# Four of six query groups in packed float32, values of two units and packed scores grouped, sink probabilities placed by VectorE, masks alone on GpSimd

## The chip, the cores and the metric

The kernel runs on one core of a Trainium2 chip. The metric is the device time of one execution in microseconds; three runs of the kernel before took 628.79 to 629.53 us, with a median of 629.14 us. Five engines share the work: TensorE (PE in the profile; PEld is its loading of weights), VectorE (DVE), ScalarE (ACT), GpSimd (POOL) and SyncE (SP, which here issues the DMAs).

## The reference

Attention with a sliding window of 128 keys and 4 sink keys, for 2 batches of 8 heads, 768 positions and a head dimension of 64, all in float32. Its output, 1536 rows of 512, goes through two feed-forward layers (512 to 2048 and back): the first with a leaky ReLU, the second with SiLU.

```python
keep = is_sink | ((rel >= 0) & (rel < window))
scores = np.where(keep, q @ k.T / sqrt(D), -1e9)
a = np.exp(scores - scores.max(-1)); a = a / (a.sum(-1) + 1e-9)
x = heads_beside_each_other(a @ v)                  # 1536 x 512
h = x @ w_in;  x = np.maximum(0.01 * h, h) @ w_out  # layer 1
h = x @ w_in2; y = (h / (1 + np.exp(-h))) @ w_out2  # layer 2
```

## The kernel before, in words

**Attention.** The 768 positions of a batch are cut into three query groups of 256, so there are six groups; `turns` puts the two first groups of the batches (g = 0, no keys before them) ahead of the other four. A unit is one pair of heads in one group: 4 units per group, 24 in all. A unit has two slots of 128 queries. `scores` (line 648) multiplies queries with at most 260 keys into the PSUM tiles `sc`; VectorE adds the mask, takes the row's extreme and writes `P`; ScalarE takes the exponential and the row's sum. `normalise` (683) divides by the sum: for g > 0 `P` itself is scaled, for g = 0 a scaled identity `by` is made, with which the transposing matmul multiplies. `transposes` (708) turns `P` around on TensorE (`tr`, for some slots the tile `h`) and ScalarE copies the result to `pT`. `values` (741) multiplies with v into the tile `at`, and ScalarE and VectorE split the result into a rounded part `xh` and its rest `xl`.

**Two forms of scores.** The first `WHOLE` = 3 groups in turn are "whole": q and k stay float32, and two heads, each 64 rows deep, are multiplied beside each other in the two halves of the array (profile form 64\*128). In the other groups q and k are split into a rounded part and a rest: ScalarE writes `qkh` (line 621), GpSimd `ql` (622), VectorE half of `qkh` (624), and the products run over 128 rows as float32r (form 128\*128). Value matmuls use half of the array's columns (128\*64). All the rest runs as 128\*128.

**Sinks.** For g > 0 the probabilities of the 4 sink keys go to `psink` as a rounded part, a rest, and the rounded part again: ScalarE, VectorE, ScalarE (703 to 705). They are transposed into `at`, and ScalarE copies two stripes of 32 rows to `sink_t` (739).

**Feed-forward.** Weights arrive as raw halves `wr` of 512 columns; ScalarE, VectorE (four operations), ScalarE and VectorE turn one into a rounded part and a rest, `w` or `we` (line 506 to 514). While attention runs, TensorE also works on 30 "items" (chunks of layer 1 for 256 positions): 12 matmuls to `h`, ScalarE and VectorE make `ga`, 12 matmuls to `ya`. After attention come 81 fused items of 512 positions: 12 matmuls to `h`, then `gb`, then 12 matmuls to four banks `y`, with `y` of an item two items behind its `h`. When a run of items over one block of positions ends, VectorE adds the four banks to `yp`.

**The order.** `Recorder` writes down every operation and then sets each engine's order by itself: it gives each operation a cost (`cost`, line 151) and a due time counted back from TensorE's order, and issues what can start first, ties by due time. Some operations may go to one of several engines (`scaled`, 235). All instructions are issued at line 441, so the profile shows that line everywhere and the names of tiles tell the operations apart.

Of the kernel before, what the change touches and what calls it, by code (L numbers as in the profile page):

```python
# [8 lines left out]
F32 = mybir.dt.float32  # L9
# [7 lines left out]
P = 128  # L17
# [4 lines left out]
WHOLE = 3  # L22
# [14 lines left out]
W_FIRST, W_EVERY = 1, 1.3  # L37

# [12 lines left out]
class View:  # L51
# [28 lines left out]

    def size(self):
        n = 1
        for a, b in self.box[1:]:
            n *= b - a
        return n
# [28 lines left out]
class Op:  # L114
    def __init__(self, eng, rank):
        self.eng, self.rank = eng, rank
        self.calls, self.cost, self.deps, self.opens, self.users = [], 0, {}, [], []
        self.bytes, self.port, self.mode = 0, False, None

        self.alts = {}  # L120


class Recorder:
# [7 lines left out]
    def __init__(self, tc):  # L131
# [3 lines left out]
        self.after = None  # L135
        for e in self.ENGINES:
            setattr(self, e, _Engine(self, e))
# [13 lines left out]
    def cost(self, eng, name, out, ins, kw):  # L151
        n = out.size() if isinstance(out, View) else 0
        psum = any(isinstance(a, View) and a.tile.pool.psum for a in [out, *ins])
        if eng == "tensor":
            passes = 4 if ins[0].dtype == F32 else 1

            half = name == "matmul" and min(out.box[0][1] - out.box[0][0], ins[0].box[0][1] - ins[0].box[0][0]) <= 64
            if name == "transpose":
                return max(109, n / 2.4)
            return n * passes / 2.4 * (0.5 if half else 1) + (20 if half else 13.3)  # L160
        if name == "dma_start":
            return 0
        if eng == "scalar":
            by = any(isinstance(kw.get(k), View) for k in ("scale", "bias"))
            sparse = isinstance(ins[0], View) and ins[0].tile.tag == "wr"
            return (182 if by else 51 if psum else 93) + n / 1.2 + (95 if "accum_out" in kw else 55 if sparse else 0)
        if eng == "vector":
# [3 lines left out]
            if name == "reciprocal":  # L171
                return 70 + n * 6
            return 68 + n / (0.96 if two or psum else 1.92)
# [15 lines left out]
    def add(self, eng, name, args, kw):  # L189
# [7 lines left out]
        else:  # L197
            op = Op(eng, self.rank - self.bias)
            op.i = len(self.ops)
            if self.after is not None:  # L200

                op.deps[self.after] = 0
            self.rank += 1
# [97 lines left out]
    def order(self):  # L301

        for op in self.ops:
            op.need, op.est = len(op.deps), 0.0
# [47 lines left out]
        while len(done) < len(self.ops):  # L352
# [33 lines left out]
            else:  # L386
                end = free[op.eng] = start + op.cost
                if op.eng == "tensor":

                    end = free[op.eng] = end + (95 if mode is not None and mode != op.mode else 0)  # L390
# [65 lines left out]
def attention_moe(ctx, tc, cfg, ins, out):  # L456
# [35 lines left out]
    def load_half(after=None):  # L492
# [5 lines left out]
        R.after = after  # L498
# [16 lines left out]
        R.after = None  # L515
# [32 lines left out]
    def emit_y(yps, gt, t, layer, c, first, last):  # L548
        cs = slice(c * P, (c + 1) * P)
        with R.group():  # L550
            for j, (a, b) in enumerate(((0, 0), (1, 0), (0, 1))):
                l, r = (wo(t, a)[:, cs], gt[:, b, :]) if layer == 0 else (gt[:, b, cs], wo(t, a))
# [4 lines left out]
    if near:  # L557
        mask = [attn.tile([P, 260], BF16, f"mask{i}") for i in range(4)]
        psink = [attn.tile([P, P], F32, f"psink{i}") for i in range(2)]
        sink_t = [attn.tile([P, GT], F32R, f"sink_t{i}") for i in range(2)]  # L560

# [40 lines left out]
    def load_qk(n):  # L602
# [19 lines left out]
        R.gpsimd.tensor_tensor(ql, raw[:, :, :GT], f32(hi[:, :, :GT]), op=ALU.subtract)  # L622
# [4 lines left out]
    def load_v(n):  # L627
# [7 lines left out]
        if d["g"] > 0 and key not in sinks:  # L635
            sr = attn.tile([P, P + 1], F32, "sr", 2)
            R.sync.dma_start(out=sr, in_=ins["vs"][key])

            sh = attn.tile([P, P], F32R, "sh", 1)
            R.vector.tensor_copy(sh, sr[:, :P])  # L640
            sinks[key] = attn.tile([P, P], F32R, "sk", NP + 1)
            R.vector.scalar_tensor_tensor(sinks[key], in0=f32(sh), scalar=sr[:, P:P + 1], in1=sr[:, :P],
# [5 lines left out]
    def scores(s):  # L648
# [10 lines left out]
        scs = {}  # L659
        if u["whole"]:  # L660

            scs = {j: ps_a.tile([P, 260], F32, "sc", 2) for j in range(2)}
            with R.group():
                for j, sc in scs.items():
# [3 lines left out]
        for j in range(2):  # L668
            if j in scs:
                sc = scs[j]  # L670
            else:
                sc = ps_a.tile([P, 260], F32, "sc", 2)
# [10 lines left out]
    def normalise(s):  # L683
# [5 lines left out]
        if d["u"]["whole"] and d["g"] == 0:  # L689

            d["by"] = attn.tile([P, 2, P], F32, "by", 3)
# [6 lines left out]
        if d["g"] > 0:  # L698
            s0 = 2 * P if i == 0 else P
            src = pt[:, :, s0:s0 + NS]  # L700
            hi, lo, hi2 = (psink[s // 2 % 2][:, o:o + 2 * NS].rearrange("p (j s) -> p j s", j=2)
                           for o in range(32 * i, 32 * i + 6 * NS, 2 * NS))
            R.scalar.activation(hi.bitcast(F32R), src, AF.Copy)
            R.vector.tensor_tensor(lo.bitcast(F32R), src, hi, op=ALU.subtract)
            R.scalar.activation(hi2, hi, AF.Copy)
        R.bias = 0

    def transposes(s):
# [16 lines left out]
        if i == 0:  # L725
            u["pT"] = attn.tile([P, 2, 512], F32, "pT", 2)
# [5 lines left out]
        u["at"] = ps.tile([P, 512], F32, "ya0", 1) if early and s // 2 % 2 else ps_a.tile([P, 512], F32, "at", 1)  # L732
        if g > 0:

            R.tensor.transpose(u["at"][:, 256:384], psink[s // 2 % 2], ident)
            st = u["st"] = sink_t[s // 2 % 2]
            for k in range(2):
                r = slice(32 * k, 32 * k + 32)
                R.scalar.activation(st[r, k * QB:(k + 1) * QB], u["at"][r, 256:384], AF.Copy)

    def values(n):

        u = state.pop(n)
        g, av, v, pT = u["g"], u["at"], u["v"], u["pT"]
        mm = [(1, 128, 384, 0), (0, 0, 128, 0), (2, 384, 512, 128)] if g > 0 else [(0, 128, 384, 0), (1, 384, 512, 128)]
        with R.group():
            if g > 0:
                R.tensor.matmul(av[:, 0:GT], sinks[u["G"] // NG, u["p"]], u["st"], start=True, stop=False)
            for k, (blk, a, e, o) in enumerate(mm):
                for j in range(2):  # L750
                    r = slice(D * j, D * j + D)
                    R.tensor.matmul(av[r, o:o + e - a], v[:, blk, r], pT[:, j, a:e],
                                    start=g == 0 and k == 0, stop=k == len(mm) - 1)
        T, t0 = divmod(u["G"] * GT, 512)
        x = [t[T][:, u["p"], t0:t0 + GT] for t in (xh, xl)]
        R.scalar.activation(x[0], av[:, 0:GT], AF.Copy)
# [294 lines left out]
```

## Time and profile before

| what | value |
|---|---|
| median of three runs | 629.14 us |
| profiled execution, its own time | 629.62 us |
| its span in the trace | 627.8 us |
| TensorE busy | 616.7 us, 98% of the span |
| VectorE, ScalarE, GpSimd busy | 400.7, 320.7, 29.4 us |
| granted TensorE clock | 1.0 (full speed) in every stretch shown |

The span begins at the first instruction and ends at the last one's end; the 1.8 us between it and the execution's own time lie outside. A busy TensorE in this profile is not TensorE at its peak: the end of a matmul is modelled, and a matmul that waits for room in the pipeline counts as busy. So for the stretch with attention one looks at the chain that ended last, and at what its pieces would take without waits.

### The profile page before, as it was taken

Reading aid. Unit: us, or ns where it says so; the run is one execution under the profiler, and the core shown is the slowest. Engines: PE = TensorE matmul, PEld = TensorE weight load, DVE = VectorE, ACT = ScalarE, POOL = GpSimd, SP = SyncE. Lnnn points to the kernel's source line nnn. Section 1 sums busy time; section 2 is a strip of 40 time slices with the busy share of each in tenths; the row PEclk is TensorE's granted clock in tenths of the full one; section 3 lists DMA queues with packets and bytes.
Section 4 is the critical chain, followed back from the end, with each engine's and each line's share of the span. In section 5 each row is a group of like instructions: output and inputs, shape, how many; then the busy total and the mean of one; then the engine's idle time right before and its main releaser. Section 6 shows DMA issues by size and latency. Waiting matters only on the chain.

```text
span 627.8 us, 9200 instructions
## 1 busy us (share of the span) xinstructions
PE 616.7 (98%) x3368; PEld 518.8 (83%) x3368; DVE 400.7 (64%) x984; ACT 320.7 (51%) x789; POOL 29.4 (5%) x44
## 2 busy tenths in 40 slices
PE   7899999999999999999999999999999999999997
PEld 5688888989998888888888888888888888888886
DVE  4998978788696666443646498874554644455254
ACT  5989999999764333332434256454323323332221
POOL 2002013320000000000000000000000000000000
PEclk9999999999999999999999999999999999999999
DMA  8544654331253212020010113220101010000013
GB/s 297 155 167 160 207 173 140 124 102 47 83 190 130 75 62 102 33 68 33 34 66 34 38 66 135 101 101 33 65 4 68 34 34 33 1 0 1 2 67 134
DMA packets 19341, 53.34 MB, mean 85 GB/s; under 512 B 2144, under 2 KB 6752, under 8 KB 19296
## 3 DMA queue, kind: packets, MB, share of 16 engines
q1 hardware_dynamic: 19296, 52.76, 24.6%
q8 instruction: 26, 0.43, 0.3%
q14 instruction: 19, 0.16, 0.1%
HBM read 49.61 MB, written 3.15 MB: 84 GB/s over the span
## 4 chain that ended last, share of the span: by engine, by line
PE 87%; ACT 10%; DVE 2%; issue 1%; DMA 0%; DVEq 0%; ACTq 0%
PE h L441 40%; PE y L441 35%; PE ya L441 5%; ACT P L441 4%; PE sc L441 3%; PE tr L441 2%; PE at L441 2%; ACT pT L441 2%; ACT qkh L441 1%; DVE P L441 1%; ACT psink L441 1%; ACT sink_t L441 1%; ACT ga L441 0%; ACT xh L441 0%; DMA qk<-in_qkd 0%
## 5 line engine op out<-in xcount | busy, mean ns | idle before, releaser
L441 PE MATMUL h<-xh,w 128*128 128x512 f32 (+1 forms) x600 | 157.2, 350 | 0.0
L441 ACT ACTIVATE g<-h 128x512 f32<-128x512 f32 (+1 forms) x111 | 59.6, 537 | 138.5 <-PE h L441 138.5
L441 PEld LDWEIGHTS h<-xh,w 128*128 128x128 f32 x600 | 104.7, 189 | 14.7 <-issue 0.8
L441 DVE TENSOR_TENSOR gb<-g,gb 128x512 fp32r<-128x512 f32 x81 | 55.9, 690 | 77.0 <-ACT g L441 61.2
L441 PE MATMUL h<-xl,w 128*128 128x512 f32 (+1 forms) x300 | 104.0, 347 | 0.0
L441 DVE TENSOR_TENSOR g<-g,h 128x512 f32<-128x512 f32 x48 | 33.0, 687 | 91.6 <-ACT g L441 91.6
L441 DVE SCALAR_TENSOR_TENSOR wb<-wr,wb 128x512 uint32<-128x512 uint32 x128 | 87.7, 689 | 2.8
L441 PE MATMUL h<-xh,we 128*128 128x512 f32 x288 | 88.7, 389 | 0.0
L441 ACT ACTIVATE gb<-h 128x512 fp32r<-128x512 f32 x33 | 19.7, 597 | 100.9 <-PE h L441 100.9
L441 PE MATMUL y<-we,gb 128*128 128x512 f32 x288 | 69.2, 389 | 0.0
L441 PE MATMUL y<-w,gb 128*128 128x512 f32 x288 | 68.9, 389 | 0.0
L441 PEld LDWEIGHTS y<-w,gb 128*128 128x128 f32 x288 | 54.1, 188 | 11.2
L441 PEld LDWEIGHTS y<-we,gb 128*128 128x128 f32 x288 | 54.1, 188 | 11.2
L441 PEld LDWEIGHTS h<-xh,we 128*128 128x128 f32 x288 | 54.1, 188 | 11.1
L441 PEld LDWEIGHTS h<-xl,w 128*128 128x128 f32 x300 | 56.7, 189 | 7.1
L441 ACT ACTIVATE P<-P,sm 128x260 f32<-128x260 f32 (+2 forms) x118 | 56.8, 492 | 7.5 <-DVE sm L441 7.3
L441 PE MATMUL y<-gb,w 128*128 128x512 f32 x252 | 60.5, 389 | 0.0
L441 PE MATMUL h<-xl,we 128*128 128x512 f32 x144 | 56.1, 390 | 0.0
L441 DVE TENSOR_SCALAR wb<-wb 128x512 f32<-128x512 f32 (+1 forms) x128 | 53.6, 424 | 3.6 <-ACT wb L441 2.2
L441 PEld LDWEIGHTS y<-gb,w 128*128 128x128 f32 x252 | 47.3, 188 | 9.8
L441 PE MATMUL ya<-ga,w 128*128 128x256 f32 x360 | 49.6, 286 | 0.0
L441 DVE TENSOR_TENSOR yp<-yp,y 128x512 f32<-128x512 f32 (+1 forms) x61 | 38.0, 673 | 14.7 <-PE y L441 14.7
(72 smaller groups left out, 767.4 us busy)
## 6 DMA issues: line engine op xcount, KB each, us to landing
wr<-in_w SPq DMA_DIRECT2D x64, 512.0 KB, 3.6
qk<-in_qkd SPq DMA_DIRECT2D x12, 644.0 KB, 3.9
v<-in_vd SPq DMA_DIRECT2D x16, 192.0 KB, 2.5
out_y<-yp SPq DMA_DIRECT2D x11, 256.0 KB, 2.1
qk<-in_qkd SPq DMA_DIRECT2D x4, 322.0 KB, 5.7
v<-in_vd SPq DMA_DIRECT2D x8, 128.0 KB, 3.5
qkh<-in_qkd SPq DMA_DIRECT2D x4, 256.0 KB, 6.7
qk<-in_qkd SPq DMA_DIRECT2D x3, 256.0 KB, 3.8
```

The source lines that it names most:

```text
L441: getattr(eng, name)(*[_real(x) for x in a], **{k: _real(x) for k, x in kw.items()})
```

## The change

- `WHOLE` goes from 3 to 4: a fourth group has packed float32 scores and no `qkh` or `ql`.
- For g = 0 both slots' scores of a unit go into one pair of PSUM banks, in one group of matmuls; units 1, 3 and 5 take the bank `ya1` for one of the pair.
- `values` handles two units at once, in one bank `at`, with one copy each to `xh` and `xl`.
- VectorE makes `sink_t` from the transposed sinks and a 0/1 mask `own`; ScalarE writes both rounded parts of `psink` in one operation.
- `ql` moves from GpSimd to VectorE, and `scaled` no longer offers GpSimd.
- The ordering gets new costs, and weight splits may not be planned more than 16 us (`HOLD`) before they are due.
- The last bank of the output is made in two halves in two banks, and the last half's store is issued by ScalarE.

```diff
-WHOLE = 3
+WHOLE = 4
+COLD = 11000
+HOLD = 16000.0
 ...
     def scaled(self, out, src, by, *more):
         self.either(("scalar", "activation", (out, src, AF.Copy), dict(scale=by)),
-                    ("vector", "tensor_scalar", (out, src, by, None), dict(op0=ALU.mult)),
-                    ("gpsimd", "tensor_scalar", (out, src, by, 1.0), dict(op0=ALU.mult, op1=ALU.mult)))
+                    ("vector", "tensor_scalar", (out, src, by, None), dict(op0=ALU.mult)))
 ...
+        for op in self.ops:
+            op.est = max(0.0, op.due - HOLD) if op.split else 0.0
 ...
-        R.gpsimd.tensor_tensor(ql, raw[:, :, :GT], f32(hi[:, :, :GT]), op=ALU.subtract)
+        R.vector.tensor_tensor(ql, raw[:, :, :GT], f32(hi[:, :, :GT]), op=ALU.subtract)
 ...
-        if u["whole"]:
-            scs = {j: ps_a.tile([P, 260], F32, "sc", 2) for j in range(2)}
+        if u["whole"] and g == 0:
+            if i == 0:
+                spare = {1: ["ya1", "sc"], 3: ["ya1", "sc"], 5: ["ya1", "sc"]}.get(s // 2, ["sc", "sc"])
+                u["sc"] = [ps_a.tile([P, 512], F32, t, 2) if t == "sc" else ps.tile([P, 512], F32, t, 1) for t in spare]
+            for blocks in ((i,),) if s < 2 else ((0, 1),) if i == 0 else ():
+                with R.group():
+                    for k in blocks:
+                        for j, sc in enumerate(u["sc"]):
 ...
-            R.scalar.activation(hi.bitcast(F32R), src, AF.Copy)
+            R.scalar.activation(twice.bitcast(F32R), src.repeat(1, [P, 2, 2, NS]), AF.Copy)
             R.vector.tensor_tensor(lo.bitcast(F32R), src, hi, op=ALU.subtract)
-            R.scalar.activation(hi2, hi, AF.Copy)
 ...
-            for k in range(2):
-                r = slice(32 * k, 32 * k + 32)
-                R.scalar.activation(st[r, k * QB:(k + 1) * QB], u["at"][r, 256:384], AF.Copy)
+            R.vector.tensor_tensor(st.rearrange("p (k n) -> p k n", k=2), u["at"][:, o:o + P].repeat(1, [P, 2, QB]),
+                                   own.rearrange("p (k n) -> p k n", k=2), op=ALU.mult)
 ...
     def values(n):
-        u = state.pop(n)
+        us = [state.pop(n + k) for k in range(2)]
 ...
+        x = [t[T][:, p:p + 2, t0:t0 + GT] for t in (xh, xl)]
+        both = av.rearrange("p (k n) -> p k n", k=2)
+        R.scalar.activation(x[0], both, AF.Copy)
+        R.vector.tensor_tensor(x[1], both, f32(x[0]), op=ALU.subtract)
 ...
+        ends = layer == 1 and final and T == NT - 1
+        parts = [(c, 0, 512) for c in range(KC - ends)] + ends * [(KC - 1, 0, 256), (KC - 1, 256, 512)]
 ...
+                R.vector.tensor_tensor(part, part, yp_k, op=ALU.add)
+                (R.scalar if o else R.sync).dma_start(out=out[r0:r0 + P, cols], in_=part)
```

On TensorE, the values of a late unit before (`at_2098` is the unit's bank; `sc` over `qkh` and `ql` are the float32r scores of the next unit):

```order
L441 MATMUL tr_2111<-ident_88,P_2008 128x128 x4
L441 MATMUL ya_5_1864<-ga_2006,w_696 128x256 x3
L441 MATMUL at_2098<-sink_t_0_138,sk_1623 128x256
L441 MATMUL at_2098<-pT_2043,v_1807 64x256 x2
L441 MATMUL at_2098<-pT_2043,v_1807 64x128 x4
L441 MATMUL sc_2145<-qkh_1957 128x260
```

On TensorE, the values of two late units in the changed kernel (`at_2054` holds both, `pT_2029` and `pT_2134` are the two units' probabilities):

```order
L463 MATMUL sc_2211<-qkh_2038 128x260
L463 MATMUL sc_2211<-qkh_2038,ql_2075 128x260
L463 MATMUL at_2054<-sink_t_0_811,sk_1015 128x256
L463 MATMUL at_2054<-sink_t_0_917,sk_1374 128x256
L463 MATMUL at_2054<-pT_2029,v_1808 64x256 x2
L463 MATMUL at_2054<-pT_2029,v_1808 64x128 x4
L463 MATMUL at_2054<-pT_2134,v_2010 64x256 x2
L463 MATMUL at_2054<-pT_2134,v_2010 64x128 x4
L463 MATMUL tr_2243<-ident_88,P_2088 128x128 x4
```

One run of half-column matmuls stands now where there were two, a unit later for the first of the pair. Over the whole program TensorE leaves the 128\*128 form 32 times instead of 38.

On ScalarE, a stretch of a late unit before (`psink` and `sink_t` are the sinks, `qkh` the split of a unit to come, `ga` and `g` belong to an item):

```order
L441 ACTIVATE psink_0_108<-P_2008 128x8
L441 ACTIVATE wb_2100<-wr_1068 128x512
L441 ACTIVATE sink_t_0_138<-at_2098 32x128 x2
L441 ACTIVATE psink_0_108<-psink_0_108 128x8
L441 ACTIVATE ga_2123<-h_2079 128x256
L441 ACTIVATE pT_2127<-tr_2111 128x2x256
L441 ACTIVATE g_2138<-h_2079 128x256
L441 ACTIVATE P_2053<-P_2053,sm_2054 128x260
L441 ACTIVATE P_2108,sm_2109<-P_2108,sm_2109 128x260
L441 ACTIVATE xh_0_1823<-at_2098 128x256
L441 ACTIVATE psink_0_108<-P_2053 128x8
```

On ScalarE, a like stretch of the changed kernel:

```order
L463 ACTIVATE pT_1911<-tr_1930 128x2x256
L463 ACTIVATE qkh_1955<-qk_69 128x1288
L463 ACTIVATE ga_1969<-h_1939 128x256
L463 ACTIVATE psink_0_106<-P_1887 128x2x8
L463 ACTIVATE P_1917<-P_1917,sm_1918 128x260
L463 ACTIVATE g_1992<-h_1939 128x256
L463 ACTIVATE P_1986,sm_1987<-P_1986,sm_1987 128x260
L463 ACTIVATE psink_0_106<-P_1917 128x2x8
L463 ACTIVATE P_1986,sm_1987<-P_1986,sm_1987 128x260
L463 ACTIVATE w_2000<-wb_1872 128x512
L463 ACTIVATE xh_0_1793<-at_1852 128x2x256
```

The `sink_t` rows and the second `psink` row of each slot are gone from ScalarE, and `xh` comes once for two units.

On VectorE, among the fused items, where the second block of positions of a pass ends, before (`yp` is the sum over banks, `gb` ends an item, `wb` to `w` is the split of weights):

```order
L441 TENSOR_TENSOR gb_3294<-g_3298,gb_3294 128x512
L441 TENSOR_TENSOR w_3303<-wb_3285,w_3303 128x512
L441 TENSOR_SCALAR wb_3326<-wb_3326 128x512 x2
L441 SCALAR_TENSOR_TENSOR wb_3326<-wr_3215,wb_3326 128x512 x2
L441 TENSOR_TENSOR yp_0_1402<-yp_0_1402,y_1_3170 128x512
L441 TENSOR_TENSOR gb_3335<-g_3339,gb_3335 128x512
L441 TENSOR_TENSOR yp_0_1402<-yp_0_1402,y_1_3178 128x512
L441 TENSOR_TENSOR yp_0_1402<-yp_0_1402,y_1_3183 128x512
L441 TENSOR_TENSOR yp_0_1402<-yp_0_1402,y_1_3187 128x512
```

On VectorE, the same place in the changed kernel:

```order
L463 TENSOR_SCALAR wb_3109<-wb_3109 128x512
L463 SCALAR_TENSOR_TENSOR wb_3085<-wr_3037,wb_3085 128x512
L463 TENSOR_SCALAR wb_3109<-wb_3109 128x512
L463 SCALAR_TENSOR_TENSOR wb_3109<-wr_3081,wb_3109 128x512
L463 TENSOR_TENSOR w_3102<-wb_3085,w_3102 128x512
L463 SCALAR_TENSOR_TENSOR wb_3109<-wr_3081,wb_3109 128x512
L463 TENSOR_SCALAR wb_3135<-wb_3135 128x512
L463 TENSOR_TENSOR yp_0_1292<-yp_0_1292,y_1_2946 128x512
L463 TENSOR_TENSOR yp_0_1292<-yp_0_1292,y_1_2953 128x512
L463 TENSOR_TENSOR yp_0_1292<-yp_0_1292,y_1_2961 128x512
L463 TENSOR_TENSOR yp_0_1292<-yp_0_1292,y_1_2966 128x512
L463 TENSOR_TENSOR gb_3141<-g_3144,gb_3141 128x512
```

The splits, held back to 16 us before they are due, stand in denser runs: between the `gb` ahead of this piece and the `gb` at its end there are nine operations on weights and four additions.

## Rows read from the trace of the kernel before

**Rows 1.** Page, busy time, share and instructions of each engine.

```profile
PE 616.7 (98%) x3368; PEld 518.8 (83%) x3368; DVE 400.7 (64%) x984; ACT 320.7 (51%) x789; POOL 29.4 (5%) x44
```

**Rows 2.** Busy time by stretch: us, PE, PEld, DVE, ACT, POOL, PEclk, DMA share, GB/s.

```profile
0.00:72.00 72.00, 66.27 (x486) 52.01 (x488) 61.25 (x264) 61.88 (x200) 9.23 (x28) 1.00 0.60 197
72.00:148.00 76.00, 74.41 (x641) 67.96 (x637) 60.76 (x230) 75.44 (x245) 19.20 (x15) 1.00 0.40 131
...
183.50:624.20 440.70, 440.70 (x1945) 364.87 (x1943) 249.04 (x418) 157.31 (x275) 0.00 (x0) 1.00 0.16 57
```

**Rows 3.** Chain that ended last, shares by engine and tile, 72 to 148 us.

```profile
by line: ACT P L441 28.0%; ACT pT L441 11.5%; ACT qkh L441 9.2%; issue 5.5%; ACT psink L441 4.7%; PE at L441 4.7%; ACT sink_t L441 4.6%; DVE P L441 4.2%; ACT ga L441 3.8%; PE ya L441 3.8%; ACT xh L441 3.6%; ACT g L441 3.1%; PE sc L441 2.4%; 
```

**Rows 4.** Chain in order of time, 0 to 185 us: start us, us, what.

```profile
35.66 0.80 PE at L441 x8
...
37.10 0.63 PE sc L441 x4
37.73 1.62 PE ya L441 x12
39.35 0.89 PE tr L441 x8
...
150.15 0.48 PE sc L441 x4
150.63 1.44 PE ya L441 x12
152.07 0.44 PE tr L441 x4
...
155.50 1.14 PE at L441 x13
```

**Rows 5.** Groups by form, 0 to 184 us: count, busy us, mean ns, idle before.

```profile
L441 ACT ACTIVATE qkh<-qk 128x1288 fp32r<-128x1288 f32 x12 | 15.3, 1276 | 0.0
...
L441 DVE TENSOR_SCALAR P<-P,sm 128x260 f32<-128x260 f32 x35 | 11.7, 358 | 0.4
...
L441 DVE TENSOR_TENSOR xl<-at,xh 128x256 fp32r<-128x256 f32 x22 | 9.2, 420 | 3.0 <-ACT xh L441 2.7
...
L441 ACT ACTIVATE xh<-at 128x256 fp32r<-128x256 f32 x22 | 8.3, 377 | 0.7 <-PE at L441 0.7
L441 ACT ACTIVATE sink_t<-at 32x128 fp32r<-32x128 f32 x32 | 8.3, 259 | 0.2
...
L441 ACT ACTIVATE psink<-P 128x8 fp32r<-128x8 f32 x32 | 6.1, 205 | 0.0
...
L441 ACT ACTIVATE psink<-psink 128x8 f32<-128x8 f32 x32 | 5.9, 207 | 0.1
...
L441 ACT ACTIVATE by<-ident,sm 128x128 f32<-128x128 f32 x7 | 2.6, 392 | 0.1
```

**Rows 6.** Instructions on the tile qkh: count, shortest, median, longest ns, first and last start.

```profile
L441 DVE TENSOR_TENSOR qkh<-qk,qkh x12: 962/964/2100, 60.5 to 137.9; 64x776 fp32r<-64x776 f32 x12
L441 POOL TENSOR_TENSOR ql<-qk,qkh x12: 1286/1296/2069, 60.6 to 137.9; 128x512 fp32r<-128x512 f32 x12
```

**Rows 7.** Chain in order of time: its start, and like matmuls early and later.

```profile
0.74 2.42 DMA qk<-in_qkd
...
9.70 2.00 PE h L441 x8
...
18.60 1.09 PE h L441 x8
```

**Rows 8.** VectorE among the fused items: start us, us, operation, idle before.

```profile
318.01 0.69 DVE L441 TENSOR_TENSOR gb<-g,gb 128x512 fp32r<-128x512 f32 x1 [2.49 <-ACT g L441]
...
324.06 0.88 DVE L441 TENSOR_SCALAR wb<-wb 128x512 f32<-128x512 f32 x2
324.97 1.42 DVE L441 SCALAR_TENSOR_TENSOR wb<-wr,wb 128x512 uint32<-128x512 uint32 x2
```

**Rows 9.** VectorE at the end of the program: start us, us, operation, idle before.

```profile
624.25 0.75 DVE L441 TENSOR_TENSOR yp<-yp,y 128x256 f32<-128x256 f32 x2 [0.67 <-PE y L441]
```

More of the change, by code (lines that the diff above doesn't have):

```diff
@@ L135, in __init__ @@
         self.after = None
+        self.splitting = False
         for e in self.ENGINES:
@@ L172, in cost @@
                 return 70 + n * 6
+            if name == "tensor_scalar" and any(isinstance(a, View) for a in ins[1:]):
+                return 128 + n / 1.92
+            if two and not psum and out.box[0][1] - out.box[0][0] <= 64:
+                return 68 + n * 1.19
             return 68 + n / (0.96 if two or psum else 1.92)
@@ L388, in order @@
                 if op.eng == "tensor":
-                    end = free[op.eng] = end + (95 if mode is not None and mode != op.mode else 0)
+                    end += 95 if mode is not None and mode != op.mode else 0
+                    end = free[op.eng] = end + min(op.cost, max(0.0, COLD - start))
                     mode = op.mode
@@ L514, in load_half @@
         R.vector.tensor_tensor(t[:, 1, cs], f32(b), f32(t[:, 0, cs]), op=ALU.subtract)
-        R.after = None
+        R.after, R.splitting = None, False
     def load_chunk():
@@ L557, in attention_moe @@
     if near:
-        mask = [attn.tile([P, 260], BF16, f"mask{i}") for i in range(4)]
+        mask = [attn.tile([P, n], BF16, f"mask{i}") for i, n in enumerate((P, 256, 260, 260))]
         psink = [attn.tile([P, P], F32, f"psink{i}") for i in range(2)]
         sink_t = [attn.tile([P, GT], F32R, f"sink_t{i}") for i in range(2)]
+        own = attn.tile([P, GT], BF16, "own")
         qk_raw = [attn.tile([P, 2, GT + 388], F32, "qk" if i < 2 else "qkh", 2) for i in range(4)]
@@ L658, in scores @@
         sm = attn.tile([P, 4], F32, "sm", 4)
-        scs = {}
-        if u["whole"]:
-            scs = {j: ps_a.tile([P, 260], F32, "sc", 2) for j in range(2)}
+        if u["whole"] and g == 0:
[6 more added lines that the diff above has]
+                        for j, sc in enumerate(u["sc"]):
+                            r = slice(D * j, D * j + D)
+                            R.tensor.matmul(sc[:, k * P:k * P + P * (k + 1)], u["raw"][r, k * QB:(k + 1) * QB],
+                                            u["raw"][r, GT:GT + P * (k + 1)], start=True, stop=True)
+                R.at_s = R.ops[-1]
+        elif u["whole"]:
+            u["sc"] = [ps_a.tile([P, 512], F32, "sc", 2) for j in range(2)]
             with R.group():
-                for j, sc in scs.items():
+                for j, sc in enumerate(u["sc"]):
                     r = slice(D * j, D * j + D)
@@ L862, in attention_moe @@
                     R.gpsimd.memset(t, 0.0)
-                for t in sink_t:
-                    for k in (0, P):
-                        R.vector.tensor_copy(t[:, k:k + P], psink[0])
+                R.gpsimd.memset(own, 1.0)
+                for k in range(2):
+                    keep_where(own[:, k * QB:(k + 1) * QB], -32 * k, 1, 0, QB, 0.0)
+                    keep_where(own[:, k * QB:(k + 1) * QB], 32 * k + 31, -1, 0, QB, 0.0)
             while halves[0] < 2 * NA and b >= W_FIRST + halves[0] * W_EVERY:
@@ L943, in fused_y @@
                 r0 = T * 512 + c * P
-                step = 256 if f == len(items) - 1 and c == KC - 1 else 512
-                for o in range(0, 512, step):
-                    e = slice(o, o + step)
-                    R.vector.tensor_tensor(part[:, e], part[:, e], yps[c][:, e], op=ALU.add)
-                    R.sync.dma_start(out=out[r0:r0 + P, e], in_=part[:, e])
+                R.vector.tensor_tensor(part, part, yp_k, op=ALU.add)
+                (R.scalar if o else R.sync).dma_start(out=out[r0:r0 + P, cols], in_=part)
     for f in range(len(items)):
```

105 lines of the change are left out of this document (61 added, 44 removed).

## The prediction

> **What bounds the kernel now.** I read the busy times first: TensorE is busy in 98% of the span [rows 1], so time can only come from work that TensorE sheds, or from its waits that this row hides. Then the stretches [rows 2]: from 183.5 us to the last matmul at 624.2 us TensorE is busy without a gap, 440.7 us for 81 fused items, 5.44 us each. The change leaves those matmuls as they are. So all that can be won lies in the first 183.5 us and in the tail. In the middle of attention, 72 to 148 us, ScalarE is busy 75.44 of 76 us, VectorE 60.76 [rows 2], and there the chain does not run along TensorE: ScalarE's groups alone (P, pT, qkh, psink, sink_t, ga, xh, g) hold 68% of it, TensorE's named ones 11% [rows 3]. ScalarE sets the pace there, though TensorE reads 74.41 us busy.
>
> How much TensorE waits I work out from what its pieces take in the chain [rows 4]. Half an item is 1.44 us, a float32r slot's scores 0.48, a packed slot's 0.63, four transposes 0.44, eight 0.89, the values of a unit 1.14 (0.80 for g = 0), and a piece that follows a run in another array form is 0.18 longer (1.62 against 1.44). The program before has 60 half items (86.4 us), 24 slots of either kind of scores (26.6 at most, since the packed slots with 128 keys are shorter), 16 and 8 units' values (24.6), 40 times four and 8 times eight transposes (24.7) and 38 runs in another form (6.8): 169 us. The first matmul starts at 3.2 us, when its data has landed [rows 7]; 183.5 less 172 is some 11 us, in which TensorE waits or is slow. In 72 to 148 us the same sum is, of 641 matmuls, 11 units of 30 matmuls (0.96 + 0.88 + 1.14 + 0.18 = 3.16 us each) and 26 half items: 72.2 us of 76, so 3.8 us of waiting. The other 7 us lie ahead of 72 us. Some of them are no wait: the eight matmuls that later take 1.09 us take 2.00 at 9.7 us [rows 7], at a time when TensorE has just begun. I put this at 3 to 4 us and leave it, since the first matmuls of the changed order depend on the same DMA.
>
> **The change part by part.** *ScalarE.* It loses 32 copies to sink_t (0.259 us), 32 second copies of psink (0.207), 4 splits qkh (1.276); 24 copies xh of 256 columns (0.377) become 12 of 512, which the table does not show on this tile; from twice 0.377 less the saved start to twice 0.377 they are 0.6 to 0.75, and I take 0.6; it gains 4 scalings by (0.392) [rows 5]. In sum 8.3 + 6.6 + 5.1 + 1.9 - 1.6 = 20 us over attention; in 72 to 148 us, with 11 units and the four splits, 5.7 + 4.6 + 5.1 + 0.8 = 16 of its 75 us. None of this is hidden work: these tiles are in the chain with 4.7, 4.6 and 9.2% [rows 3].
>
> *VectorE.* It gains 16 sink_t (like an xl of 256 columns from PSUM, 0.42 [rows 5]; not faster than the 0.36 of the scaling of 260 columns and not slower than the 0.69 of 512 columns [rows 8]; I take 0.42, the nearest shape), 8 ql of 512 columns (0.69 [rows 8]) and 7 scalings (0.358 [rows 5]); it loses 4 halves of qkh (0.96 [rows 6]) and some 1.8 us of xl. That is 6.7 + 5.5 + 2.5 - 3.8 - 1.8 = 9 us more over attention, some 8 of them in 72 to 148 us: 69 of 76 us. GpSimd and VectorE also stood in each other's way: the same half of qkh took 0.96 to 2.10 us on VectorE, the same ql 1.29 to 2.07 on GpSimd [rows 6]; with GpSimd making masks only, this goes, which I count as cover for the estimate and not as a term. So ScalarE falls to 59 of 76 us, VectorE rises to 69, and TensorE with 72 becomes the bound. ql comes earlier for the scores, since it takes 0.69 instead of 1.3 us; but it and sink_t now queue on VectorE behind the mask additions of the next slots, and TensorE waits for both.
>
> *TensorE.* Eight slots of scores go from 0.48 to 0.63 us and bring a run in another form each: 8 times 0.33 is 2.6 us more [rows 4]. Values in pairs and grouped scores for g = 0 take out 14 runs at 0.18 us, and at most some 0.1 us each for seven entries: 2.5 to 3.2 us less. In sum -0.6 to +0.1; I take -0.5, since the order shows 38 runs fall to 32.
>
> The page TensorEngine Tiling (Array Packing) of the Trainium skill, under Tiling Modes, says that changing the tiling mode drains TensorE, while changing the tile within a mode does not. The 0.18 us agree. By that rule alone the fourth packed group is a loss of TensorE's own time, and the gain would have to come from pairing; with the eight new runs alone and no pairing the sum would be 3.1 us worse.
>
> *What returns of the waits.* In 72 to 148 us there are 3.8 us of waiting to be had; with ScalarE at 78% I expect some 3.0 back, not all, because the order is fixed and VectorE at 90% will make TensorE wait now and then. Ahead of 72 us VectorE is busy 61.25 and ScalarE 61.88 of 72 us [rows 2]: no engine there is freed by much, the grouped scores give VectorE more to do at once, but pairing delays the first unit's xh until the second's probabilities are there. Bounds are a gain of 3.5 (all but the slow start) and a loss of 2.3 (the second unit's scores, transposes and values, 0.63 + 0.89 + 0.80 us [rows 4], ahead of the first xh); I take a gain of 1.0, nearer to the middle than to the upper end.
>
> *Weights.* HOLD moves splits behind; it takes no instruction away. Attention needs 15 halves in either order. Among the fused items VectorE is busy 249 of 441 us [rows 2], so a delay is hidden as long as a dense run doesn't outlast its lead; that is a rival below. I cost it at nothing.
>
> *The tail.* The last two additions take 0.75 us together after the last matmul [rows 9]; with the halves in two banks the first runs beside matmuls: 0.35 us less, between 0 and 0.4.
>
> The sum: 3.0 + 1.0 + 0.5 + 0.35 is 4.85 us off the profiled execution's 629.62, so 624.8. That execution was 0.5 us above the median; against the median of 629.14 this gives 624.3.
>
> **Rivals.** *VectorE takes ScalarE's place.* Moving 8 to 9 us onto it makes 69 of 76 us, and ql and sink_t stand directly before matmuls. For it: VectorE serves every score tile in order. Against it: ScalarE could run at 99%, and 69 us is less than TensorE's 72. Then the waits stay and only half the early gain, the pairing and the tail are won: 627.2 to 629.5 us.
>
> *All waits go.* If VectorE and ScalarE both keep ahead, TensorE wins back up to 11 us less the slow start, and the 0.85: from 621.5 down to 617.4 us, the floor if even the slow start went. Against it speaks that a set order keeps some waits.
>
> *Held-back splits stall the fused items: slower.* In the changed order VectorE has nine operations on weights, four additions and a gb between two neighbouring gb: by [rows 8] 2 times 0.69, 4 times 0.71, 3 times 0.44 and 5 times 0.69 are 9.0 us, against 5.44 for TensorE's item: 3.6 us behind. The gb itself has room: between an item's h and its y stand two whole items, 10.9 us, of which ScalarE and VectorE need some 2. The four additions have less, since y of the next block of positions starts one h, 2.7 us, after the last y, and needs the banks empty. About seven such dense runs stand in the order. If each costs 2 us, attention's 4.85 us are turned into 9 us of loss: 638; at 1.4 us each 634. From 0.7 us each on it decides. Against it: the order before had additions among splits too, and TensorE never waited there.
>
> *No effect.* The waits may hang on the probabilities' chain (mask, exponential, sum, scaling, transposition), which the change leaves as long as it was; with the pairing as gain and a later first xh as loss the time stays within 0.2%, 627.9 to 630.4 us, about what a measurement of this kernel can tell from no change.
>
> **How the numbers follow.** The forecast, 621.5 to 627.2 us, has 0.55; VectorE as the bound 0.17, half of it within 0.2%; all waits gone 0.14; stalled fused items 0.09; no effect 0.05. Faster: 0.55 + 0.09 + 0.14 = 0.78. Same: 0.08 + 0.05 = 0.13. Slower: 0.09. The range from 618.8 to 628.8 us leaves out the stalls, the lowest part of the floor case and half of the no-change cases, under 2 in 10.
>
> **What the profile after would show.** Right: in the middle of attention ScalarE under 85% busy, VectorE near 90%, and the chain along TensorE's h, ya, sc, at; the last values end some 4 us earlier; the fused items still 5.44 us each; one addition of 0.4 us after the last matmul. Wrong: a chain full of VectorE's sink_t, ql and P (first rival), or gaps in TensorE after the start of the fused items with yp or gb as the releaser (third), or the first h of an item later than before by more than the pairing wins.

## The result, and the profile after

The changed kernel takes 623.99 us (median of 4 runs, 623.87 to 625.37) against 629.34 us for the kernel before beside it (628.79 to 631.55): a ratio of 0.9917, 95% interval 0.9899 to 0.9934. A second set of six runs gave 624.54 us and 0.9927 (0.9910 to 0.9944). The forecast was 624.3 us, with a range of 618.8 to 628.8. The execution profiled below took 625.37 us with a span of 623.6 us, the longest of its four (the others 622.1 to 622.3), so the traces show 4.2 us of the gain.

Busy times of the changed kernel on the page, answering to [rows 1]:

```profile
PE 611.6 (98%) x3374; PEld 516.3 (83%) x3374; DVE 397.1 (64%) x995; ACT 309.4 (50%) x713; POOL 5.0 (1%) x26
```

The same stretches as in [rows 2] (us, PE, PEld, DVE, ACT, POOL, granted clock, DMA share, GB/s); the last one runs from the first matmul of the fused items to the end of the last:

```profile
0.00:72.00 72.00, 63.20 (x488) 51.23 (x489) 61.27 (x261) 58.86 (x187) 4.99 (x26) 1.00 0.66 213
72.00:148.00 76.00, 76.00 (x667) 69.00 (x666) 63.84 (x253) 70.06 (x205) 0.00 (x0) 1.00 0.30 98
179.50:620.40 440.90, 440.90 (x1952) 365.18 (x1951) 247.55 (x427) 162.10 (x279) 0.00 (x0) 1.00 0.17 58
```

In the middle TensorE is now busy for all 76 us (74.41 before), ScalarE for 70.06 (75.44), VectorE for 63.84 (60.76). Ahead of 72 us TensorE is busy less than before, 63.20 against 66.27. The 81 fused items take what they took: 440.90 us, 440.70 before. The chain that ended last, 72 to 148 us, answering to [rows 3]:

```profile
by line: PE ya L463 26.6%; PE h L463 24.4%; PE at L463 18.9%; PE sc L463 16.2%; PE tr L463 14.0%
```

It runs along TensorE alone; ScalarE's 68% of [rows 3] are gone. Attention is over sooner: the last values end at 159.3 us (163.1 before), the fused items start at 179.55 (183.4). Groups of attention by form (count, busy us, mean ns), answering to [rows 5]:

```profile
L463 DVE TENSOR_TENSOR xl<-at,xh 128x512 fp32r<-128x512 f32 x11 | 7.5, 686 | 2.2 <-ACT xh L463 2.2
...
L463 DVE TENSOR_TENSOR sink_t<-at,own 128x256 fp32r<-128x256 f32 x16 | 6.6, 414 | 0.0
L463 ACT ACTIVATE psink<-P 128x16 fp32r<-128x16 f32 x32 | 6.6, 212 | 0.8 <-DVE P L463 0.3 <-DVE sm L463 0.2
L463 ACT ACTIVATE xh<-at 128x512 fp32r<-128x512 f32 x11 | 6.4, 586 | 1.7 <-PE at L463 1.7
...
L463 DVE TENSOR_TENSOR ql<-qk,qkh 128x512 fp32r<-128x512 f32 x8 | 5.5, 685 | 0.0
```

Each is within 0.02 us of the duration that the prediction gave it. VectorE at the end (start us, us, operation, idle before), answering to [rows 9]:

```profile
619.06 1.14 DVE L463 TENSOR_TENSOR yp<-yp,y 128x512 f32<-128x512 f32 x2 [0.67 <-PE y L463]
620.49 0.42 DVE L463 TENSOR_TENSOR yp<-yp,ya 128x256 f32<-128x256 f32 x1 [0.29 <-PE ya L463]
```

One addition of 0.42 us follows the last matmul, where two took 0.75 together.

What went the other way lies ahead of 72 us. ScalarE (first fence) and TensorE (second fence) of the changed kernel, in order of time:

```profile
13.37 0.67 ACT L463 ACTIVATE wb<-wr 128x512 f32<-128x512 f32 x1 [1.09 <-DMA wr<-in_w]
...
15.47 0.58 ACT L463 ACTIVATE pT<-h 128x512 f32<-128x512 f32 x1
...
40.29 0.66 ACT L463 ACTIVATE wb<-wr 128x512 f32<-128x512 f32 x1 [1.77 <-DMA wr<-in_w]
40.85 0.59 ACT L463 ACTIVATE pT<-tr 128x512 f32<-128x512 f32 x1
```

```profile
16.10 0.87 PE L463 MATMUL at<-pT,v 128*64 128x256 f32 x8 [1.07 <-ACT pT L463]
...
41.49 0.71 PE L463 MATMUL tr<-by,P 128*128 128x128 f32 x4 [1.36 <-ACT pT L463]
```

ScalarE reaches wb, its share of a weight split, before the weights have landed. It stands 1.09 and 1.77 us, the pT queued behind it comes late, and TensorE stands 1.07 and 1.36 us for that pT. ScalarE has no less to do here than before, 33.58 against 33.37 us up to 42 us; it is the new order that sets its first two shares of splits earlier, at 11.12 and 13.37 us. In the kernel before they start later and wait for nothing:

```profile
13.90 0.66 ACT L441 ACTIVATE wb<-wr 128x512 f32<-128x512 f32 x1
...
16.63 0.66 ACT L441 ACTIVATE wb<-wr 128x512 f32<-128x512 f32 x1
```

### The profile page after: what moved, and what is told of

It is laid out like the page before. It is cut to its first block, busy times and chain, and to the rows that moved or that the text cites. A ratio compares the mean times of both kernels' runs of the same rounds, so it can differ in the third digit from the quotient of the medians.

```text
span 623.6 us, 9092 instructions
## 1 busy us (share of the span) xinstructions
PE 611.6 (98%) x3374; PEld 516.3 (83%) x3374; DVE 397.1 (64%) x995; ACT 309.4 (50%) x713; POOL 5.0 (1%) x26
## 4 chain that ended last, share of the span: by engine, by line
PE 93%; ACT 3%; DMA 3%; issue 0%; SPq 0%; DVE 0%; ACTq 0%
PE h L463 42%; PE y L463 35%; PE ya L463 7%; PE at L463 3%; PE sc L463 3%; PE tr L463 3%; DMA wr<-in_w 2%; ACT P L463 1%; DMA qk<-in_qkd 1%; ACT pT L463 1%; ACT wb L463 1%; ACT by L463 0%; SPq L463 0%; ACT w L463 0%; ACT xh L463 0%
## 5 line engine op out<-in xcount | busy, mean ns | idle before, releaser
L463 DVE SCALAR_TENSOR_TENSOR wb<-wr,wb 128x512 uint32<-128x512 uint32 x128 | 86.0, 685 | 1.0
L463 PE MATMUL y<-w,gb 128*128 128x512 f32 (+1 forms) x288 | 68.2, 387 | 0.0
L463 PEld LDWEIGHTS ya<-ga,w 128*128 128x128 f32 x360 | 45.3, 190 | 3.4 <-issue 2.4
```

The lines of the kernel that those rows point to most:

```text
L463: getattr(eng, name)(*[_real(x) for x in a], **{k: _real(x) for k, x in kw.items()})
```

## The experiments

Every ratio is to the kernel before, run beside it on the same chip. The two measurements of the changed kernel give a gain of 0.83 and 0.73%; where a price for undoing a part is stated, it is the difference to their mean, 0.78% (4.9 us). Differences under some 1 us lie within the intervals. The ends of units are read where TensorE leaves their values for the next piece: unit 12 ends at 78.8 us before and 79.0 in the changed kernel, unit 24 at 163.1 and 159.3.

**Sinks back on ScalarE.** Both copies to sink_t per unit and the second copy of psink return; all else is as changed.

```diff
-            R.vector.tensor_tensor(st..., u["at"][:, o:o + P].repeat(1, [P, 2, QB]), own..., op=ALU.mult)
+            for k in range(2):
+                r = slice(32 * k, 32 * k + 32)
+                R.scalar.activation(st[r, k * QB:(k + 1) * QB], u["at"][r, o:o + P], AF.Copy)
...
-            R.scalar.activation(twice.bitcast(F32R), src.repeat(1, [P, 2, 2, NS]), AF.Copy)
+            R.scalar.activation(hi.bitcast(F32R), src, AF.Copy)
...
+            R.scalar.activation(hi2, hi, AF.Copy)
```

> The changed kernel with the sinks as before: ScalarE writes sink_t in two copies and the second rounded part of psink by itself. ScalarE does 48 operations more (some 11 to 15 us over attention), VectorE 16 less (5 to 7 us). Theory (ScalarE's share is what was won): 626 to 627.5. Rival (the gain is from the new order and from TensorE's fewer changes of form): 623.5 to 624.5.

Measured: 627.30 us, ratio 0.9957 (0.9941 to 0.9972). Its middle stretch and its chain there:

```profile
72.00:148.00 76.00, 75.49 (x649) 67.38 (x647) 59.83 (x236) 72.53 (x238) 0.00 (x0) 1.00 0.28 90
```

```profile
by line: ACT P L463 12.5%; PE h L463 11.3%; PE ya L463 9.9%; ACT qkh L463 9.4%; PE at L463 8.6%; PE sc L463 7.4%; ACT pT L463 6.2%; PE tr L463 5.3%; DVE P L463 3.6%; ACT psink L463 3.2%; ACT ga L463 2.7%; issue 2.7%; DVE qkh L463 2.5%; DMA 
```

ScalarE is back at 72.53 us, TensorE waits again, and ScalarE's P, qkh, pT and psink are in the chain. Unit 12 ends at 79.1 us and unit 24 at 161.5, so the 2.2 us are lost between them. The move of the sinks is worth 0.35% of the time, 2.2 us, within the changed order. The theory held.

**The sink edit alone,** put into the kernel before (with the mask `own` and, as in the changed kernel, one buffer less for the loads of the sinks).

```diff
-            R.scalar.activation(hi2, hi, AF.Copy)
...
-            for k in range(2):
-                r = slice(32 * k, 32 * k + 32)
-                R.scalar.activation(st[r, k * QB:(k + 1) * QB], u["at"][r, 256:384], AF.Copy)
+            R.vector.tensor_tensor(st..., u["at"][:, 256:384].repeat(1, [P, 2, QB]), own..., op=ALU.mult)
```

> The kernel before with the sinks' edit alone: VectorE makes sink_t, ScalarE writes both rounded parts at once. Theory (ScalarE alone sets the pace from 72 to 148 us): ScalarE loses some 10 us there, at most 3.8 us of waiting are to be had, so 1.5 to 3.5 us faster than before, 626 to 627.8. Rival (the pieces of the change only work together, since the order is what counts): within 0.8 us of before.

Measured: 628.63 us, ratio 0.9992 (0.9978 to 1.0005): nothing that can be told from no change. Its middle stretch and chain:

```profile
72.00:148.00 76.00, 74.39 (x647) 68.36 (x646) 70.45 (x252) 72.41 (x215) 17.81 (x16) 1.00 0.44 146
```

```profile
by line: DVE P L445 14.5%; PE ya L445 13.2%; PE h L445 13.2%; PE at L445 10.3%; PE tr L445 8.0%; PE sc L445 7.0%; DVE qkh L445 6.4%; ACT P L445 4.9%; DVE wb L445 4.1%; issue 3.0%; DVE psink L445 2.3%; DVE sm L445 2.2%; DVE ga L445 2.2%; DVE
```

ScalarE fell by 3 us against [rows 2], but VectorE rose from 60.76 to 70.45, twice what the products cost. Groups on VectorE there (count, busy us, mean ns):

```profile
L445 DVE SCALAR_TENSOR_TENSOR wb<-wr,wb 128x512 uint32<-128x512 uint32 x10 | 6.8, 680 | 0.0
...
L445 DVE TENSOR_TENSOR sink_t<-at,own 128x256 fp32r<-128x256 f32 x11 | 4.5, 412 | 0.0
```

Most of the rest is weight splits: ten operations of this form lie in the stretch, four in the kernel before and in the changed one. The chain went over to VectorE's P. TensorE is busy 74.39 us, as before. The rival held. This is the prediction's first rival, in a kernel without the other parts.

**Splits not held back.**

```diff
-            op.est = max(0.0, op.due - HOLD) if op.split else 0.0
+            op.est = 0.0
```

> The changed kernel without HOLD: weight splits may be planned as early as their data allows. Theory (splits are hidden work, before attention's end or after): 623.5 to 624.8, no change. Rival 1 (holding back frees ScalarE and VectorE during attention): 625.5 to 627. Rival 2 (dense late splits cost TensorE waits among the fused items): under 623.

Measured: 628.25 us, ratio 0.9974 (0.9959 to 0.9988): holding the splits back is worth 0.52%, 3.3 us. Not all of it is the splits' own room. In eight of the twelve runs, the profiled one among them, TensorE's granted clock has a mean of 0.997 over the execution, in one of ten runs of the changed kernel; the last section shows where it falls. The other four have a median of 626.6 us, 2.4 us above the 624.2 of the changed kernel's other nine. The stretch from 50 to 100 us of this kernel, and then of the changed one:

```profile
50.00:100.00 50.00, 48.99 (x397) 40.93 (x396) 48.65 (x189) 45.01 (x134) 0.00 (x0) 1.00 0.53 171
```

```profile
50.00:100.00 50.00, 50.00 (x408) 42.06 (x407) 41.58 (x175) 43.05 (x132) 0.00 (x0) 1.00 0.40 128
```

Without it VectorE is full, 48.65 of 50 us against 41.58, and TensorE waits. ScalarE's wb pays too (count, busy, mean ns, idle before), in this kernel and in the changed one:

```profile
L463 ACT ACTIVATE wb<-wr 128x512 f32<-128x512 f32 x20 | 13.5, 681 | 9.0 <-DMA wr<-in_w 9.0
```

```profile
L463 ACT ACTIVATE wb<-wr 128x512 f32<-128x512 f32 x20 | 13.3, 676 | 4.6 <-DMA wr<-in_w 4.6
```

It stands 9.0 us for weights that haven't landed, instead of 4.6. That HOLD costs and gives nothing was wrong; of the expectations the first rival, that ScalarE and VectorE are freed, comes nearest.

**Values of one unit at a time.**

```diff
...
-                if b % 4 == 2:
-                    values(b // 2 - 3)
+                values(b // 2 - 2)
```

> The changed kernel with the values of one unit at a time, as before: some 12 runs in half-column form more on TensorE at 0.18 us, xh and xl in 24 pieces instead of 12. Theory: TensorE has 2.2 us more to do and is the bound, so 625.5 to 627. Rival (pairing delays the first xh as much as it saves): 623 to 624.5.

Measured: 626.73 us, ratio 0.9949 (0.9933 to 0.9965). Pairing is worth 0.27%, 1.7 us. From 72 to 148 us TensorE is busy throughout in this kernel too and the chain runs along TensorE alone, so no wait shows there and the price is put down to TensorE's own work, 12 runs in half-column form more, 0.14 us each. Unit 12 ends at 79.0 us, as in the changed kernel, unit 24 at 161.2. The theory held.

**Three packed groups instead of four,** measured twice, the second time beside the changed kernel.

```diff
-WHOLE = 4
+WHOLE = 3
```

> The changed kernel with three groups packed instead of four, all else as changed. Theory (ScalarE's relief lets TensorE work, TensorE is the bound): ScalarE gets 4 qkh splits (5.1 us) back, VectorE some, TensorE loses eight packed slots at 0.33 us (2.6 us); with ScalarE still under 90% busy the time is 622.5 to 625, about the changed kernel's 624.0. Rival (the fourth packed group is what relieved the engines): 626 to 628.

> The changed kernel with three packed groups, a second time, beside the changed kernel. Theory (eight packed slots cost TensorE 0.33 us each and ScalarE no longer needs their relief): 1.5 to 3 us faster than the changed kernel, 621.5 to 623. Rival (the first runs differed by the chip alone): within 0.6 us of it.

Measured: 623.24 us, ratio 0.9892 (0.9875 to 0.9910), and 623.41 us, 0.9905 (0.9887 to 0.9923), against 624.54 and 0.9927 for the changed kernel beside the second:

> The changed kernel as it is, to stand beside the kernels of this call. Both theories: 623.9 to 624.6, as in its first runs.

The middle stretch of the second of these runs, and its chain:

```profile
72.00:148.00 76.00, 75.14 (x672) 70.94 (x673) 68.26 (x262) 73.01 (x213) 0.00 (x0) 1.00 0.38 124
```

```profile
by line: PE h L463 16.6%; PE ya L463 15.1%; ACT P L463 11.3%; PE at L463 9.6%; PE sc L463 7.8%; PE tr L463 7.5%; DVE P L463 5.9%; ACT pT L463 3.8%; DVE qkh L463 3.8%; ACT qkh L463 3.1%; DVE ql L463 2.5%; DVE sm L463 1.8%; DVE xl L463 1.6%; 
```

ScalarE and VectorE do more here, 73.01 and 68.26 us, and TensorE waits 0.9 of 76 us for them. Yet the last values end at 157.05 us instead of 159.3. Some 1.0 us of these 2.25 is idle time: up to 160 us TensorE stands 7.8 us here and 8.8 in the changed kernel. From 40 to 50 us the two read, this one first:

```profile
40.00:50.00 10.00, 10.00 (x78) 8.07 (x79) 10.00 (x35) 8.91 (x28) 0.00 (x0) 1.00 0.46 146
```

```profile
40.00:50.00 10.00, 8.64 (x68) 6.88 (x68) 9.02 (x30) 8.93 (x27) 0.00 (x0) 1.00 0.37 115
```

The weights that ScalarE met too early at 40.29 us in the changed kernel have nearly landed when it comes to them here, and pT is not held up:

```profile
38.61 0.68 ACT L463 ACTIVATE wb<-wr 128x512 f32<-128x512 f32 x1 [0.29 <-DMA wr<-in_w]
39.20 0.58 ACT L463 ACTIVATE pT<-tr 128x512 f32<-128x512 f32 x1
```

The rest, some 1.2 us, is left for TensorE's shorter scores, less than the 2.6 us of eight slots. It is the fastest version tried, by 1.1 us beside the changed kernel; the intervals overlap, the two measurements agree in sign.

**Three groups, the first units' values singly.**

```diff
...
+                if b // 2 - 2 < 2 * NP:
+                    values(b // 2 - 2, 1)
+                elif b % 4 == 2 and b // 2 - 3 >= 2 * NP:
...
```

> Three packed groups, and the values of g = 0 units one at a time, those of the others in pairs. Theory (pairing the first units delays the first xh and so the first item by some 1.5 us, while the four runs saved there are worth 0.7 us): 0.5 to 1.5 us faster than three packed groups alone. Rival (the early stretch is bound by VectorE and the start, not by xh): the same or up to 1 us slower, for the four runs in half-column form more.

Measured: 625.05 us, ratio 0.9929 (0.9914 to 0.9944), 1.6 us behind three groups with all values paired, though its first item starts as early (27.56 us, 27.65 paired). Pairing the first units is no loss: the theory fell, and the price is above the rival's 1 us.

**First group's scores not grouped.** The block that packs scores of g = 0 for two heads into one group goes; the older branch serves all packed slots.

```diff
-        if u["whole"] and g == 0:
...
-        elif u["whole"]:
+        if u["whole"]:
```

> The changed kernel with the scores of the two slots of g = 0 units in their own banks and groups, as before. Theory (seven runs in packed form more, 0.18 to 0.28 us each, in a stretch where VectorE and ScalarE are full as well): 624.3 to 626. Rival (grouping delays the first transposes as much as it saves): 623 to 624.3.

Measured: 629.96 us, ratio 1.0008 (0.9998 to 1.0019). The whole gain is lost, more than any theory said. Matmuls of this kernel in order of time, and then of the changed one:

```profile
8.67 2.05 PE L463 MATMUL h<-by,P 128*128 128x128 f32 x8 [0.27 <-DVE by L463]
...
16.16 2.08 PE L463 MATMUL h<-by,P 128*128 128x128 f32 x8 [0.19 <-ACT by L463]
...
18.90 2.20 PE L463 MATMUL at<-pT,v 128*64 128x256 f32 x16
...
22.21 1.06 PE L463 MATMUL h<-by,P 128*128 128x128 f32 x8
```

```profile
8.65 1.72 PE L463 MATMUL h<-by,P 128*128 128x128 f32 x8
...
11.71 1.06 PE L463 MATMUL h<-by,P 128*128 128x128 f32 x8
```

Eight transposes take 2.08 us as late as 16.16 us, against 1.06 at full pace; in the changed kernel the full pace is there by 10 us. The first pair of values ends at 21.03 us instead of 16.91, the first item starts at 31.24 instead of 27.83. The profiled execution is the shortest of its twelve, 628.70 us, and 3.3 us longer than the changed kernel's: the 3.4 us at the first item account for that. The other 2 us between the medians show in no trace.

**ScalarE burdened:** the second pT copy of each unit done twice, 24 more copies, some 11.5 us.

```diff
+        R.scalar.activation(u["pT"][:, :, (i + 1) * 256 - n:(i + 1) * 256],
+                            tr[:, 0:2 * n].rearrange("p (j n) -> p j n", j=2), AF.Copy)
```

> The changed kernel with one copy of each unit's second pT done twice: 24 operations of 0.48 us (0.59 as the profile shows them), some 11.5 us more on ScalarE over attention, nothing else. Theory (ScalarE now has some slack, but little): part of it comes through, 625.5 to 628. Rival (ScalarE was never the bound): under 624.8.

Measured: 628.50 us, ratio 0.9987 (0.9974 to 1.0000), 4.1 us worse than the changed kernel. Here too ten of the twelve runs have a mean granted clock of 0.994 to 0.997; the two others take 626.19 and 626.95 us, some 2.4 us above the changed kernel. In the profiled execution unit 12 ends 1.9 us later than in the changed kernel and unit 24 2.5 us later, so most of the loss lies at the start; from 72 to 148 us TensorE is busy 75.85 of 76 us.

**VectorE burdened:** the sink product done three times, 32 more of 0.34 us, some 11 us.

```diff
+            for _ in range(2):
+                R.vector.tensor_tensor(st..., u["at"][:, o:o + P].repeat(1, [P, 2, QB]), own..., op=ALU.mult)
```

> The changed kernel with each sink_t product done three times instead of once: 32 operations of 0.34 us (0.42 as the profile shows them), some 11 us more on VectorE in the eighteen units with sinks' stretch, 50 to 160 us. Theory (VectorE is at 80 to 90% there and TensorE is the bound): 624.3 to 626. Rival (VectorE has become the bound): 628 or more.

Measured: 626.00 us, ratio 0.9953 (0.9936 to 0.9970), 2.0 us worse, with all nine runs at 0.999 or 1.00. That a like burden costs twice as much on ScalarE does not show that ScalarE has the smaller reserve: ScalarE's extra copies lie in all 24 units, VectorE's products only in the 16 with sinks, and without the runs at a lower clock the prices are 2.4 (two runs) and 2.0 us.

**GpSimd computes again:** ql there, and it may take scalings.

```diff
-        R.vector.tensor_tensor(ql, raw[:, :, :GT], f32(hi[:, :, :GT]), op=ALU.subtract)
+        R.gpsimd.tensor_tensor(ql, raw[:, :, :GT], f32(hi[:, :, :GT]), op=ALU.subtract)
...
+                    ("gpsimd", "tensor_scalar", (out, src, by, 1.0), dict(op0=ALU.mult, op1=ALU.mult)))
```

> The changed kernel with ql on GpSimd again and GpSimd allowed for scalings. Theory: GpSimd takes some 15 us of work off VectorE, which is not the bound, and the two slow each other; ql comes 0.6 us later: 624 to 625. Rival (VectorE is now the bound): faster than the changed kernel by over 0.5 us, 622 to 623.4.

Measured: 624.44 us, ratio 0.9910 (0.9895 to 0.9926): no difference. Its ql takes 1285 to 2085 ns on GpSimd, against 685 on VectorE, and TensorE is busy for 76.00 of 76 us in the middle in this kernel as well. Who computes ql makes no difference to the time here.

## Why the prediction was right

*What bounds the kernel.* Right. With ScalarE relieved the chain of the middle runs along TensorE alone; with the sinks back on ScalarE TensorE is busy 75.49 of 76 us and ScalarE is in the chain again. That VectorE would take ScalarE's place did not come true in this kernel (63.84 of 76 us, not 69): with the splits held back it had room, which the sink edit alone shows from the other side.

*Middle waits, 3.0 us.* Right in kind. From the end of unit 12 to the end of unit 24 it is 84.3 us before and 80.3 after, 4.0 less. How much of it is waits, no row shows. As an estimate I compared each step from one piece of TensorE's order to the next with its usual length: the excess falls by some 3 to 4 us, depending on what is taken as usual.

*Early stretch, a gain of 1.0 us.* Wrong in sign for the profiled execution: ahead of 72 us TensorE stands idle 8.80 us instead of 5.73, the first item starts 1.5 us later (27.83 us, 26.36 before), and unit 12 ends 0.2 us later. The price I feared, pairing, is at most a part of it: with all values singly the first item starts at 27.11 us, with the first units' alone at 27.56, and the latter is 1.6 us slower. The rows show ScalarE standing at wb for weights, and pT behind it; where the weights had landed, with three groups, TensorE had no gap from 40 to 50 us. That this accounts for all of it was not tried.

*TensorE's work, 0.5 us.* Too small, though its size is a remainder. With 3.1 us more of idle time ahead of 72 us TensorE has done as many matmuls there (488, 486 before), so they took less time. A part of this is the slow start, which the prediction left as it was because the first matmuls depend on the same DMA: it became shorter. Four transposes before and in the changed kernel:

```profile
12.36 1.22 PE L441 MATMUL tr<-by,P 128*128 128x128 f32 x4
```

```profile
11.16 0.71 PE L463 MATMUL tr<-by,P 128*128 128x128 f32 x4
```

Undoing the pairing costs 1.7 us. The 0.18 us for a run in another form comes from two rows of the chain, which go from end to end; from start to start a half item behind packed scores takes 1.53 us against 1.44, which is half of that, while undoing the pairing's 12 runs cost 0.14 each.

*The fourth packed group, 2.6 us.* The prediction set this against the removed runs and let it pass. The runs with three groups put it at a loss of 1.1 to 1.5 us net. Attention ends 2.25 us sooner there in the traces, 1.0 of it by less idle time, although ScalarE and VectorE are busier. By the rule that the prediction cites from the Trainium skill (TensorEngine Tiling (Array Packing), Tiling Modes), that a change of mode drains TensorE, the group was a loss too; the runs agree in sign, but do not separate the changes of mode from the longer scores.

*Weights at nothing.* Wrong: 3.3 us hang on HOLD, 2.4 at full clock. The sum didn't suffer, because the prediction took VectorE to have room for the moved work, and HOLD is what gives it that room. The rival that held-back splits stall the fused items is refuted: 440.90 us without a gap.

*The tail, 0.35 us.* Right: the last matmul ends 3.76 us earlier, the span 4.2 us, which leaves 0.44.

*ScalarE under 85%, VectorE near 90%.* Wrong: 92 and 84%. ScalarE lost 5.4 us there, not 16. Groups of the middle stretch (count, busy us, mean ns, idle before), ScalarE's before:

```profile
L441 ACT ACTIVATE P<-P,sm 128x260 f32<-128x260 f32 x57 | 28.3, 509 | 0.1
L441 ACT ACTIVATE qkh<-qk 128x1288 fp32r<-128x1288 f32 x11 | 14.0, 1275 | 0.0
```

ScalarE's in the changed kernel, then VectorE's before and in the changed kernel:

```profile
L463 ACT ACTIVATE P<-P,sm 128x260 f32<-128x260 f32 x63 | 31.6, 507 | 4.5 <-DVE sm L463 3.6 <-DVE psink L463 0.8
...
L463 ACT ACTIVATE qkh<-qk 128x1288 fp32r<-128x1288 f32 x8 | 10.2, 1278 | 0.0
```

```profile
L441 DVE TENSOR_TENSOR qkh<-qk,qkh 64x776 fp32r<-64x776 f32 x11 | 12.6, 1142 | 1.2 <-ACT qkh L441 0.7
L441 DVE TENSOR_SCALAR P<-P,sm 128x260 f32<-128x260 f32 x28 | 9.3, 360 | 0.4
```

```profile
L463 DVE TENSOR_SCALAR P<-P,sm 128x260 f32<-128x260 f32 x29 | 9.6, 352 | 0.4
L463 DVE TENSOR_TENSOR qkh<-qk,qkh 64x776 fp32r<-64x776 f32 x8 | 7.7, 964 | 1.3 <-ACT qkh L463 1.2
```

I had given the scalings that GpSimd loses to VectorE; ScalarE has six P of 0.5 us more, VectorE one. Of the splits qkh three fall away in this stretch, not four. And counting with mean durations was wrong: ScalarE's operations overlap in the records, so that its groups of this stretch add up to 97 us where it is busy 75.44, and a short copy that goes frees less than its own duration (32 copies of 0.207 us in psink are 5.9 us busy in [rows 5], not 6.6). And the halves of qkh, 12.6 us before (eleven of 1142 ns on average), are 7.7: the slowing by GpSimd that [rows 6] show, which I didn't count, made up 2.0 us of that (11 times 1142 less 964 ns).

So the sum was right because of errors of opposite sign, and that is luck: up to the end of unit 12 nothing was won (0.2 us lost), where the forecast had 1.0 us and a part of TensorE's 0.5; from there to the end of unit 24 it was 4.0 us, where it had 3.0 and the rest. The prices of the parts do not add up: sinks 2.2, pairing 1.7, HOLD 3.3 and grouped scores 5.4 make 12.6 us, against 4.9 for the whole. Each is a price within an order that was planned anew around what is left. Open is how the early loss divides between the weights' landing, the qk transfers and run-to-run differences. Untried are the new costs of the ordering by themselves, COLD among them, the two halves of the last bank, and a third buffer for pT, which the change brings too and the list of its parts leaves out.

## What to carry to other kernels

Relief of one engine can be used up by other work that a planner puts in its place: the sink edit alone won nothing, and in the changed kernel, with the splits held back, it is worth 2.2 us (the sink edit with HOLD and nothing else was not tried). In these rows ScalarE's pT came late behind a wb that waited for a transfer, so check, when an order is planned anew, which transfers an engine now reaches too early. Take the relief of an engine from its busy time, not from the sum of mean durations. And weigh each part against the engine that will be the bound afterwards: the fourth packed group relieved two engines that TensorE waited for 0.9 of 76 us, and burdened TensorE, which was the bound.

## What the runs showed of the hardware

TensorE's slow start is not of fixed length. In the changed kernel matmuls come to full pace by 10 us, with scores not grouped only around 20 us, in the kernel before between 12.4 and 15 us, and the granted clock reads 1.00 there throughout, the level of 2.4 GHz. Ahead of the early rise the changed kernel has TensorE at work from 7.64 us until then without a gap; the one with scores not grouped has gaps of 0.2 to 0.4 us between its pieces.

A second effect is in the granted clock itself. The second profiled execution of the changed kernel, 12 to 25 us (the columns of the windows above):

```profile
12.00:15.00 3.00, 1.98 (x16) 1.46 (x14) 2.19 (x11) 1.84 (x4) 0.00 (x0) 1.00 1.03 399
15.00:18.00 3.00, 1.95 (x15) 1.07 (x16) 2.33 (x12) 3.00 (x12) 0.00 (x0) 0.84 0.93 351
18.00:21.00 3.00, 3.00 (x20) 2.55 (x16) 3.00 (x16) 2.60 (x11) 0.00 (x0) 0.59 0.86 285
21.00:25.00 4.00, 3.88 (x35) 2.88 (x36) 3.55 (x18) 3.94 (x12) 0.00 (x0) 1.00 0.55 167
```

TensorE is busy 1.98 and 1.95 of 3 us, waiting 1.02 us for VectorE's sm and 1.05 for pT, and then the granted clock falls to a mean of 0.84 and 0.59, between the levels of 2.4 and 1.2 GHz, until 21 us. The first execution is busy 2.86, 1.80 and 2.27 of 3 us in the same three stretches and keeps 1.00. The first pair ends at 18.51 us in the one and 16.91 in the other, with the same order of instructions: part of the spread of 2 us between runs of this kernel. The profiled executions without HOLD and with ScalarE burdened show the same fall at the same place, to 0.71 and 0.73 and to 0.89 and 0.54 in 15 to 18 and 18 to 21 us, after TensorE was busy 2.47 and 1.81 of 3 us from 12 to 15. In these two kernels most runs have a lower mean clock, in the changed kernel one of ten, so a delay of the first units can cost time twice there, in the wait and in the clock behind it.
